# Three of seven gate/up tile pairs as seven products of halves (256 of 448 channels), with the roundings moved behind PSUM copies and the inverse transform split around the down projection

## The chip, the cores and the metric

The kernel runs on one core of a Trainium2 chip. The metric is the device time in microseconds. The kernel before was run three times: 1939.03, 1943.02 and 1942.74 us, median 1942.74 us. A further execution, taken with the hardware profiler, is the one whose trace is read here.

TensorE is called PE, VectorE DVE, ScalarE ACT, GpSimd POOL, and SP is the engine that issues the DMAs. "PEld" is PE's weight load.

## The reference

An input of 8192 rows by 448 channels goes through a spectral block and then a feed-forward block, each behind a modulated layer norm and with a gated residual:

```
h = _layernorm(x) * (1 + ca) + sa
x = x + ga * _A_ref(h, ...)                  # rfft2, two block-diagonal complex layers, softshrink, irfft2
h = _layernorm(x) * (1 + cb) + sb
x = x + gb * (gelu(h @ w_gate) * (h @ w_up)) @ w_down     # 448 -> 1792 -> 448
```

The case turns on the last line. It is done with float16 operands in two parts: a high part and the remainder, for weights and activations both, so one product takes three matmuls (high by high, high by low, low by high).

## The kernel before, in words

The first 380 us or so do the Fourier transform and the block-diagonal layers. What follows is one loop over `nch` = 32 chunks of 256 tokens (`for i in range(nch)`, L1275), each in 14 steps `k`.

**Gate and up.** A step is one 128-wide block of the hidden features. Steps 2t and 2t+1 (`q` = 0 and 1) make tile pair t, with t from 0 to 6; here it is called pair t. A step runs 20 matmuls of 256 columns (L1087): gate and up, each with ten weight blocks. The 448 channels lie in four weight blocks, the last of 64 rows. The products of those 64 rows with the low weights are taken together for two neighbouring pairs, eight matmuls of half height, at the end of the second step of the first of the two (`first_pair`, L1099).

**PSUM banks.** A first pair has two banks with the tag "pa", a second pair two with the tag "pb" (L1100 to L1103); each tag has two buffers, so the same two banks serve every second pair. The first write to the new "pa" banks is at the beginning of a first pair's steps, the first write to the new "pb" banks is among the eight half-height matmuls just named. Because a chunk has seven pairs, an odd chunk begins with a second pair and ends with one (pair 6 uses "pb"), and an even chunk ends with a first pair (pair 6 uses "pa").

**After a step.** `gate_up_out` (L1120) takes the gelu of the gate half on ACT (L1123, into one of two `gel` buffers) and multiplies by the up half on DVE (L1128); both read the PSUM bank, and the bank can be written again after the multiplication. For a second pair this follows each step, for a first pair both follow its second step. POOL then makes four sums of 128x128 (L1134 to L1137). `quantize` rounds the seven blocks to float16 on ACT (L1145) and takes the remainder on DVE (L1146).

**Down.** After step 2 of a chunk, `down` (L1158) runs the projection of the chunk before it, in seven products of halves instead of eight (147 matmuls of 224 columns), with sums on ACT, DVE and POOL, and stores the chunk.

**Preparation of chunk i+2.** The `hooks` table (L1201) spreads it over the steps of chunk i: the last inverse transform (L987 to L989, operands split into two parts by ACT and POOL, L105 and L107), the residual (L998 and L999), the row statistics (L1007), a reciprocal square root in 14 tiny DVE instructions (L116 to L125), the norm (L1036 and L1037), and the float16 packing (L1042, L1049 to L1051). Sixteen DMA transposes (L1057) follow a chunk later.

Each engine works through its instructions in the order in which the program wrote them, so an instruction that waits holds up what stands behind it on its engine.

Of the kernel before, what the change touches and what calls it, by code (L numbers as in the profile page):

```python
# [37 lines left out]
NTT = len(PKO)  # L38
LAM = 0.01
# [6 lines left out]
def spectral_geglu(ctx, tc, x, w1, b1, w2, b2, wg, wu, wd, cvec, wmod, cf1, cs2, cmi, cgm, out):  # L46
# [272 lines left out]
    with ExitStack() as bctx:  # L319
# [359 lines left out]
        def row_scales():  # L679
# [8 lines left out]
            pow2(sk, bnd)  # L688
# [50 lines left out]
        def scales1():  # L739
# [20 lines left out]
            pow2(sw, mxa)  # L760
# [122 lines left out]
        def load_g(i):  # L883
            g = ep.tile([128, CB, 128], F32, tag="g", name="g")
            dma(g, cgm[:, i * CB : (i + 1) * CB, :])
            xx = ep.tile([128, CB, D], F32, tag="xx", name="xx")
            dma(xx, xv[:, i * CB : (i + 1) * CB, :])
            nxt.setdefault(i, {}).update({"g": g, "xx": xx})
# [22 lines left out]

        def split_g(i):
            gh = ep.tile([128, CB, 128], F32R, tag="gh", name="gh")
            gl = ep.tile([128, CB, 128], F32R, tag="gl", name="gl")
            split(gh, gl, nxt[i]["g"], el=G)
            nxt[i]["g"] = gh, gl
# [32 lines left out]
    with ExitStack() as cctx:  # L949
# [7 lines left out]

        def load_d8(t):
            load_d(t, *(cp2.tile([128, n, HC], F32, tag=f"dr{n}", name="dr", bufs=2) for n in (3, 4)))
# [8 lines left out]
        def split_v(i, cs=slice(0, D)):  # L968
            n = nxt[i]
            if "vh" not in n:  # L970
                n["vh"] = cp.tile([128, CB, D], F32R, tag="vh", name="vh")
                n["vl"] = cp.tile([128, CB, D], F32R, tag="vl", name="vl")
            for b in each(i):
                split(n["vh"][:, b, cs], n["vl"][:, b, cs], n["v"][:, b, cs], el=G)

        def inverse(i, cs=slice(0, D), tag="pc"):
            nxt[i]["ps"] = []
            for b in range(CB):
                ps = bank(tag, "pi2")[:, cs]
                if i < 3:  # L980

                    T.matmul(ps, nxt[i]["g"][:, b], nxt[i]["v"][:, b, cs], start=True, stop=True)
                    nxt[i]["ps"].append(ps)
                    continue
                vh, vl = nxt[i]["vh"], nxt[i]["vl"]
                gh, gl = nxt[i]["g"]
                T.matmul(ps, gh[:, b], vh[:, b, cs], start=True, stop=False)  # L987
                T.matmul(ps, gl[:, b], vh[:, b, cs], start=False, stop=False)  # L988
                T.matmul(ps, gh[:, b], vl[:, b, cs], start=False, stop=True)  # L989
                nxt[i]["ps"].append(ps)  # L990

        def residual(i, cs=slice(0, D)):
# [383 lines left out]
```

## Time and profile before

| | before |
|---|---|
| median of three runs | 1942.74 us |
| the profiled execution | 1942.27 us |
| its span in the trace | 1940.5 us |
| mean granted PE clock | 0.995 |
| PE busy | 1901.1 us (98%) |
| DVE busy | 1108.7 us (57%) |
| ACT busy | 790.1 us (41%) |
| POOL busy | 1157.7 us (60%) |

The busy time is a mean over the whole program; the loop over chunks, from about 400 us on, is the part that the change touches. A timeline row gives the start, the time to the end of the last of the merged instructions, the engine, the line, and how many were merged; in brackets stands the idle time before, and what ended it. A group row gives the number of instructions, their busy time together, and the mean duration of one. Durations of one engine overlap by a little, so what an instruction costs in a dense row is the distance to the next start.

### The profile page before, as it was taken

The page shows a single profiled execution, that of the slowest core. Times are in us where ns is not written, and L with a number is a line of the kernel's source. Part 1 is how long each engine was busy: PE and PEld are TensorE (multiplying, and loading weights), DVE is VectorE, ACT ScalarE, POOL GpSimd, SP SyncE. Part 2 cuts the span into 40 slices and gives each one's busy share as a digit, 9 for nine tenths or more (in the row PEclk, how much of TensorE's full clock was granted, in tenths as well). Part 3 has the DMA queues.
Part 4 walks back from the last instruction along what each step waited for, and adds up shares of the span by engine and source line. Part 5 has one row for each costly group of instructions (what it writes and reads, how often), then busy time and mean ns, then how long its engine had stood idle before and what let it go on. Part 6 is the DMA issues. An engine that isn't in the chain of part 4 may idle for free.

```text
span 1940.5 us, 43566 instructions
## 1 busy us (share of the span) xinstructions
PE 1901.1 (98%) x17636; PEld 1694.6 (87%) x17636; DVE 1108.7 (57%) x2352; ACT 790.1 (41%) x1342; POOL 1157.7 (60%) x1466
## 2 busy tenths in 40 slices
PE   7899999899999999999999999999999999999998
PEld 3599999778888888888888888888888888888897
DVE  8677788786555555555555555555555555555533
ACT  5587888553333333333333333333333333333322
POOL 3157655256666666666666666666666666666644
PEclk9899999999999999999999999999999999999999
DMA  9999777541111111111111111111111111111000
GB/s 351 313 286 261 194 195 196 166 125 48 44 44 44 43 43 43 43 43 44 43 44 43 43 44 43 44 44 42 45 43 44 44 43 44 43 44 44 21 16 20
DMA packets 167330, 163.35 MB, mean 84 GB/s; under 512 B 87252, under 2 KB 145496, under 8 KB 167128
## 3 DMA queue, kind: packets, MB, share of 16 engines
q1 hardware_dynamic: 167128, 160.57, 28.3%
q8 instruction: 138, 2.26, 0.5%
q14 instruction: 64, 0.52, 0.1%
HBM read 97.44 MB, written 47.25 MB: 75 GB/s over the span
## 4 chain that ended last, share of the span: by engine, by line
PE 86%; DVE 4%; ACT 3%; issue 3%; DMA 2%; POOL 1%; SPq 1%; ACTq 0%; POOLq 0%; DVEq 0%
PE pgu L1087 53%; PE pdn L1155 8%; PE pdn L1153 8%; PE pdn L1154 8%; PE ps L202 2%; DVE y L463 2%; PE pi L989 1%; PE pi L988 1%; PE pi L987 1%; POOL yl L107 1%; DVE st L163 1%; ACT th L105 0%; DMA raw<-in_B_w_gate 0%; POOL tl L107 0%; ACT zh L376 0%
## 5 line engine op out<-in xcount | busy, mean ns | idle before, releaser
L1087 PE MATMUL pgu<-nt,wh 128*128 128x256 f16 x6272 | 834.2, 273 | 0.1
L1087 PEld LDWEIGHTS <-wh 128*128 128x128 f16 x6272 | 602.7, 98 | 98.5 <-issue 31.0
L1123 ACT ACTIVATE gel<-pgu,dg 128x256 f32<-128x256 f32 x448 | 200.3, 473 | 793.2 <-PE pgu L1087 756.1
L1087 PE MATMUL pgu<-nt,wl 128*128 128x256 f16 (+1 forms) x3584 | 501.3, 272 | 0.6 <-DVE x L1128 0.6
L1155 PE MATMUL pdn<-wd,ac 128*128 128x224 f16 x1568 | 406.1, 259 | 0.2 <-DVE ac L1146 0.2
L1153 PE MATMUL pdn<-wd,ac 128*128 128x224 f16 x1568 | 406.1, 259 | 0.0
L1154 PE MATMUL pdn<-wd,ac 128*128 128x224 f16 x1568 | 406.1, 259 | 0.0
L1134 POOL TENSOR_TENSOR x<-x 128x128 f32<-128x128 f32 x223 | 239.9, 1076 | 264.0 <-DVE x L1128 230.5
L1146 DVE SCALAR_TENSOR_TENSOR ac<-x,sa_act,ac 128x896 f16<-128x896 f32 (+1 forms) x225 | 308.2, 1370 | 81.9 <-ACT ac L1145 81.9
L1087 PEld LDWEIGHTS <-wl 128*128 128x128 f16 (+1 forms) x3584 | 297.8, 97 | 57.6 <-issue 24.4
L1128 DVE TENSOR_TENSOR x<-pgu,gel 128x256 f32<-128x256 f32 x448 | 179.6, 418 | 278.7 <-ACT gel L1123 278.0
L1145 ACT ACTIVATE ac<-x,sa_act 128x896 f16<-128x896 f32 (+1 forms) x225 | 232.9, 1035 | 46.5 <-POOL x L1137 44.5
L1190 POOL TENSOR_TENSOR o<-u,p 128x224 f32<-128x224 f32 x32 | 21.0, 657 | 291.6 <-DVE u L1189 291.6
L1135 POOL TENSOR_TENSOR x<-x 128x128 f32<-128x128 f32 x223 | 158.1, 709 | 17.5
L1155 PEld LDWEIGHTS <-ac 128*128 128x128 f16 x1568 | 153.4, 98 | 0.5 <-DVE ac L1146 0.5
L1154 PEld LDWEIGHTS <-ac 128*128 128x128 f16 x1568 | 153.4, 98 | 0.4
L1153 PEld LDWEIGHTS <-ac 128*128 128x128 f16 x1568 | 153.4, 98 | 0.4
L107 POOL TENSOR_TENSOR yl<-y,yh 128x448 fp32r<-128x448 f32 x63 | 78.9, 1252 | 75.6 <-ACT yh L105 63.0
L463 DVE SCALAR_TENSOR_TENSOR y<-pm,t 64x224 f32<-64x224 f32 x256 | 99.5, 389 | 41.3 <-ACT t L455 37.4
L1136 POOL TENSOR_TENSOR x<-x 128x128 f32<-128x128 f32 x223 | 113.0, 507 | 0.0
L1137 POOL TENSOR_TENSOR x<-x 128x128 f32<-128x128 f32 x223 | 109.2, 490 | 0.0
L107 POOL TENSOR_TENSOR tl<-tr,th 128x896 f16<-128x896 f32 x30 | 57.3, 1909 | 69.5 <-DMA tr<-td 38.2
(281 smaller groups left out, 2728.4 us busy)
## 6 DMA issues: line engine op xcount, KB each, us to landing
tr<-td SPq DMA_DIRECT2D x64, 224.0 KB, 4.3
vd<-us SPq DMA_DIRECT2D x64, 224.0 KB, 3.3
xx<-in_A_x SPq DMA_DIRECT2D x32, 448.0 KB, 3.3
v<-vd SPq DMA_DIRECT2D x63, 224.0 KB, 2.7
out<-x SPq DMA_DIRECT2D x31, 448.0 KB, 2.6
xt<-in_A_x SPq DMA_DIRECT2D x15, 896.0 KB, 14.8
td<-xt SPq DMA_DIRECT2D x48, 224.0 KB, 4.3
nt<-pk SPq DMA_TRANSPOSE x480, 2.3
```

What stands on the lines that cost most here:

```text
L107: (el or V).tensor_tensor(lo, src, h, ALU.subtract)
L463: V.scalar_tensor_tensor(y[ri * 64 : ri * 64 + 64, gi], pv[si, ri], LAM, tv[si, ri], op0=ALU.add, op1=ALU.min)
L1087: T.matmul(pgu[i, t, q][:, pr * H : (pr + 1) * H], w[rows, tw, f0 : f0 + 128], nts[i][rows, tn, :], start=start, stop=stop, skip_group_che ...
L1123: S.activation(gl, ps[:, :H], AF.Gelu_apprx_tanh, scale=dg)
L1128: V.tensor_tensor(dst, ps[:, H : 2 * H].rearrange("p (b c) -> p b c", b=2), gl.rearrange("p (b c) -> p b c", b=2), ALU.mult)
L1134: e.tensor_tensor(s1, a21, a22, ALU.add)
L1135: e.tensor_tensor(s2, s1, a11, ALU.subtract)
L1145: S.activation(ac[:, 0, k], x[:, k], AF.Copy, scale=sc)
L1146: V.scalar_tensor_tensor(ac[:, 1, k], x[:, k], sc, ac[:, 0, k], op0=ALU.mult, op1=ALU.subtract)
L1153: T.matmul(ps, ac[:, 0, ka], wds[t][:, 0, kb], start=t == 0, stop=False)
L1154: T.matmul(ps, ac[:, 0, ka], wds[t][:, 1, kb], start=False, stop=False)
L1155: T.matmul(ps, ac[:, 1, ka], wds[t][:, 0, kb], start=False, stop=t == NP - 1)
```

## The change

For pairs 2, 4 and 6, from chunks 3, 4 and 5 on (`SP`), the part of gate and up over the first two weight blocks (256 channels) is written as a 2x2 block product, two halves of the channels by two halves of the features and of the tokens, and taken in seven products instead of eight. Each product is 128x128x128 for gate and for up, so its matmuls have 128 columns. The other two weight blocks stay as they were (`rest`, with 256 columns). The core of it:

```diff
+        def gate_up_s1(i, t, first_pair):
+            pv = bank("pc", "px").rearrange("p (x r c) -> p x r c", x=2, r=2)
+            x, u = pv[:, 0], sums["u"]
+            sp_product(i, t, x, 0, 0, start=True)
+            sp_product(i, t, pv[:, 1], 3, 3)
+            S.copy(u[:, :, 0], x)
+            rest(i, t, 0, 0, first_pair, 2)
+            sp_product(i, t, x, 4, 6)
+            S.copy(u[:, :, 1], x)
+            rest(i, t, 0, 1, first_pair, 2)
+            o = outs(i, t, 0)
+            sp_product(i, t, o[:, :, 0], 1, 1, stop=not first_pair)
+            sp_product(i, t, x, 5, 4, stop=True)
+            S.copy(u[:, :, 2], x)
+            sp_product(i, t, o[:, :, 1], 2, 5, stop=not first_pair)
+        def gate_up_s2(i, t, first_pair):
+            for pr in range(2):
+                rest(i, t, 1, pr, first_pair, 2)
+            sp_product(i, t, outs(i, t, 1)[:, :, 0], 6, 2, stop=not first_pair)
...
             if not first_pair:
+                gate_up_sums(i, t, q)
                 gate_up_out(i, t, q)
...
+        def gate_up_sums(i, t, q):
+            if seven(i, t):
+                u, o = sums["u"], outs(i, t, q)
+                if q == 0:
+                    V.tensor_tensor(o, o, u[:, :, 0::2], ALU.add)
+                    y = sums["px"][:, 1].unsqueeze(2).broadcast_to([128, 2, 2, 128])
+                    V.tensor_tensor(u[:, :, 1:3], y, u[:, :, 1:3], ALU.add)
+                else:
+                    V.tensor_tensor(o, o, u[:, :, 1:3], ALU.add)
...
-                if k % 2 == 1 and i + k > 1 and (i, k) != (nch - 1, NFT - 1):
-                    quantize(*((i, k // 2 - 1) if k > 1 else (i - 1, NP - 1)))
+                for p in [p for p in unrounded if 2 * p + 3 + (p >= 2 * NP) == i * NFT + k]:
+                    quantize(*divmod(p, NP))
...
         hooks = {
-            0: [(1, transposes_dma)],
-            3: [(2, split_g), (2, split_v)],
-            6: [(2, inverse)],
-            7: [(2, residual)],
-            8: [(2, stats2)],
-            9: [(2, rsqrt_part, 5)],
+            0: [(1, transposes_dma, range(4))],
+            3: [(1, s_transposes), (2, inverse1, 0), (2, split_v, 1)],
+            4: [(2, residual, slice(0, D), [0])],
+            5: [(2, stats2, slice(0, D), [0])],
+            6: [(2, inverse1, 1)],
+            7: [(2, residual, slice(0, D), [1])],
+            9: [(2, stats2, slice(0, D), [1]), (2, rsqrt_part, 5)],
             10: [(2, rsqrt_part, 9)],
             11: [(2, norm2, 0)],
             12: [(2, norm2, 1)],
-            13: [(2, pack_hi), (2, pack_lo)],
+            13: [(2, pack_hi), (2, pack_lo), (2, s_sums)],
         }
```

One product (`sp_product`) is six matmuls of 128 columns: gate and up, three each. A pair has 42 of them, 36 in its first step (with `px`, a bank of tag "pc", for the partial sums that more than one output needs) and six in its second. ACT copies the running partial sum out of `px` three times (`u`), and PE adds to `px` after the first and after the second copy. DVE adds the copies to the output banks, two instructions of 128x512 after the first step and one after the second; for a first pair all three follow the second step.

Further: POOL makes four sums and one remainder for the activations of the seven products, and ACT one copy (`s_sums`, `s_pack`); eight more DMA transposes per chunk carry them (`s_transposes`). `quantize` comes one step later, at even steps instead of odd ones. The inverse transform of a chunk is taken one half of the chunk at a time (`inverse1`), the first after step 3, the second after step 6; the splitting of its operands begins inside `down`. The norm writes into the tile that held the transform's input, so the loads for chunk i+2 move from the steps 0 and 1 to step 2, and the load of `x` behind `down`. The weights' sums are made once per pair, in chunks 2 to 4. Two scale factors become smaller by four, with no change in work.

The first place is DVE, from the multiplication after step 11 of an odd chunk to the multiplication after step 13. `pgu` is an output bank, `x` with a number a pair's tile (25719 and 28330 are pair 5, 25756 and 28393 pair 6), `ac` the float16 result, `dr` the copies `u`. Before:

```order
L1128 TENSOR_TENSOR x_25719<-pgu,gel 128x256
L1146 SCALAR_TENSOR_TENSOR ac<-x_25611,sa_act,ac 128x896
L1036 SCALAR_TENSOR_TENSOR n_25731<-x_25584,cmv,cb_r 128x448
L1037 SCALAR_TENSOR_TENSOR n_25731<-n_25731,rcy,sb_r 128x448
L1128 TENSOR_TENSOR x_25756<-pgu,gel 128x2x128
L1036 SCALAR_TENSOR_TENSOR n_25731<-x_25584,cmv,cb_r 128x448
L1037 SCALAR_TENSOR_TENSOR n_25731<-n_25731,rcy,sb_r 128x448
L1128 TENSOR_TENSOR x_25756<-pgu,gel 128x256
```

And the same stretch after the change:

```order
L1271 TENSOR_TENSOR x_28330<-pgu,gel 128x256
L1039 SCALAR_TENSOR_TENSOR v<-x_28075,cmv,cb_r 128x448
L1040 SCALAR_TENSOR_TENSOR v<-v,rcy,sb_r 128x448
L1257 TENSOR_TENSOR pgu<-pgu,dr 128x512
L1259 TENSOR_TENSOR dr<-px,dr 128x2x256
L1271 TENSOR_TENSOR x_28393<-pgu,gel 128x2x128
L1289 SCALAR_TENSOR_TENSOR ac<-x_28228,sa_act,ac 128x896
L1039 SCALAR_TENSOR_TENSOR v<-x_28075,cmv,cb_r 128x448
L1040 SCALAR_TENSOR_TENSOR v<-v,rcy,sb_r 128x448
L1261 TENSOR_TENSOR pgu<-pgu,dr 128x512
L1271 TENSOR_TENSOR x_28393<-pgu,gel 128x256
```

Three additions of 128x512 have come between (L1257, L1259, L1261), and the remainder for pair 4 (`x_25611`, `x_28228`) has moved from behind pair 5's multiplication to behind pair 6's first one.

The second place is ACT in the same odd chunk, from the gelu of pair 5 to the packing after step 13. Before:

```order
L1123 ACTIVATE gel<-pgu,dg 128x256 x2
L1145 ACTIVATE ac<-x_25611,sa_act 128x896
L1123 ACTIVATE gel<-pgu,dg 128x256 x2
L1145 ACTIVATE ac<-x_25719,sa_act 128x896
L1042 CAST pk<-n_25731 128x2x448
```

After:

```order
L1266 ACTIVATE gel<-pgu,dg 128x256 x2
L1210 COPY dr<-px 128x2x128
L1213 COPY dr<-px 128x2x128
L1218 COPY dr<-px 128x2x128
L1266 ACTIVATE gel<-pgu,dg 128x256
L1288 ACTIVATE ac<-x_28228,sa_act 128x896
L1266 ACTIVATE gel<-pgu,dg 128x256
L1045 CAST pk<-v 128x2x448
```

The three copies out of `px` stand behind both gelus of pair 5 and ahead of the gelu and the rounding that follow.

More of the change, by code (lines that the diff above doesn't have):

```diff
@@ L995, in residual @@
             x1 = x1t[i][:, :, cs]
-            for b in range(CB):
+            for b in bs:
                 e = V if i < 3 else G
@@ L1241, in spectral_geglu @@
         }
+        for i in (1, 2):
+            x1t[i] = x1_tile(i)
+        nxt[0]["n"] = x1t[2]
         inverse(0, halves[0], "pa")
@@ L1274, in spectral_geglu @@
         V.tensor_scalar(gb_r, gb_r, ds_d, None, op0=ALU.mult)
+        unrounded = range(nch * NP - 2)
         for i in range(nch):
```

204 lines of the change are left out of this document (158 added, 46 removed).

## The prediction

> **What bounds the kernel now.** I read the stages first, then PE's timeline, then what PE waits for. In the loop over chunks the columns after the window's length are the busy time of PE, PEld, DVE, ACT and POOL:
>
> ```profile
> 1000.00:1200.00 200.00, 200.00 (x1913) 178.64 (x1911) 107.28 (x220) 64.88 (x108) 129.50 (x167) 1.00 0.16 44
> ```
>
> PE has no gap at all there, at full granted clock (1.00), while DVE and ACT are busy for 54% and 32%. So time is won by fewer PE columns, and lost as soon as any engine makes PE wait. The end of an odd chunk on PE:
>
> ```profile
> 1050.22 0.94 PE L1087 MATMUL pgu<-nt,wh 128*128 128x256 f16 x7
> ...
> 1054.60 0.93 PE L1087 MATMUL pgu<-nt,wh 128*128 128x256 f16 x7
> ...
> 1058.64 1.03 PE L1087 MATMUL pgu<-nt,wl 128*128 128x256 f16 x11
> 1059.61 0.94 PE L1087 MATMUL pgu<-nt,wh 128*128 128x256 f16 x7
> ```
>
> Step 12 begins at 1050.22, the next (even) chunk two steps later at 1054.60: a step is 2.19 us for 20 matmuls, 0.109 us each. The row at 1058.64 holds three whole matmuls (to 1058.97) and the eight half-height ones, 0.08 us each. From the third of them, at 1059.13, PE writes the "pb" banks that pair 6 used. DVE at the same time:
>
> ```profile
> 1047.15 0.63 DVE L1007 BATCH_NORM_STATS2 cst<-x 128x6 f32<-128x448 f32 x1 [0.47 <-POOL x L999]
> 1047.70 0.30 DVE L1010 BATCH_NORM_AGGREGATE cmv<-cst 128x2 f32<-128x6 f32 x2
> 1047.91 0.39 DVE L1128 TENSOR_TENSOR x<-pgu,gel 128x256 f32<-128x256 f32 x1
> 1048.22 1.14 DVE L1146 SCALAR_TENSOR_TENSOR ac<-x,sa_act,ac 128x896 f16<-128x896 f32 x1
> 1049.28 0.42 DVE L116 TENSOR_SCALAR rcve<-cmv 128x2 f32<-128x2 f32 x1
> ...
> 1052.35 0.75 DVE L1128 TENSOR_TENSOR x<-pgu,gel 128x256 f32<-128x256 f32 x2
> 1053.01 1.14 DVE L1146 SCALAR_TENSOR_TENSOR ac<-x,sa_act,ac 128x896 f16<-128x896 f32 x1
> 1054.07 0.88 DVE L1036 SCALAR_TENSOR_TENSOR n<-x,cmv,cb_r 128x448 f32<-128x448 f32 x1
> 1054.98 0.76 DVE L1037 SCALAR_TENSOR_TENSOR n<-n,rcy,sb_r 128x448 f32<-128x448 f32 x1
> 1055.67 0.41 DVE L1128 TENSOR_TENSOR x<-pgu,gel 128x256 f32<-128x256 f32 x1
> ...
> 1057.59 0.42 DVE L1128 TENSOR_TENSOR x<-pgu,gel 128x256 f32<-128x256 f32 x1
> ```
>
> The mean of 54% hides this: from 1047.15 on DVE never stops, and pair 6's last multiplication ends at 1058.01, only 1.1 us ahead of PE's write at 1059.13. An even chunk has its pair 6 in "pa", written next at the beginning of step 2 (first row DVE, second PE):
>
> ```profile
> 1105.09 0.74 DVE L1128 TENSOR_TENSOR x<-pgu,gel 128x256 f32<-128x256 f32 x2
> ```
> ```profile
> 1107.60 0.93 PE L1087 MATMUL pgu<-nt,wh 128*128 128x256 f16 x7
> ```
>
> Its multiplications end at 1105.83: 1.8 us to spare. That PE does wait for this multiplication when it is late, the list of PE's waits shows once:
>
> ```profile
> PE pgu L1087 <- DVE x L1128: 0.6, 1, 0.6
> ```
>
> **What the change saves.** Per changed pair 24 matmuls of 256 columns go and 42 of 128 columns come. Such matmuls with a weight load each exist already, in the Fourier stage (24 of them, first and last shown) and in the first transposes, with full 128x128 weights:
>
> ```profile
> 250.84 0.22 PE L368 MATMUL ps<-s,th 128*112 128x128 f16 x1
> ...
> 252.13 0.22 PE L370 MATMUL ps<-s,tl 128*112 128x128 f16 x1
> ```
> ```profile
> 383.59 0.61 PE L1069 MATMUL ptr<-ident,pk 128*128 128x128 f16 x8
> ```
>
> 1.29 us over 23 intervals is 0.056 us each; the eight transposes give (0.61 - 0.22)/7 = 0.056 too. So a pair costs 42 x 0.056 = 2.36 us in place of 24 x 0.109 = 2.62, a saving of 0.26 us. Pairs 2, 4 and 6 are changed from chunks 3, 4 and 5 on: 29 + 28 + 27 = 84 pairs, **-21.8 us**. A changed pair's first step is then 36 x 0.056 + 8 x 0.109 = 2.89 us, its second 6 x 0.056 + 8 x 0.109 = 1.21.
>
> The Trainium skill, "TensorE: Matmul & The Clock Gate", section "Back-to-back issue gap", speaks against this: in a stream of weight loads and matmuls it gives about 81 ns for N=128, and 56 ns only for an isolated gap. By it a pair would take 42 x 0.081 = 3.40 us, a loss of 0.79 us, an estimate of +66 us for 84 pairs; the rows above, which are such streams, measure 56 ns, and the sum goes by them.
>
> **What the sums on DVE cost.** No 128x512 addition is in the trace. The nearest rows are group rows (count, total, mean ns):
>
> ```profile
> L1128 DVE TENSOR_TENSOR x<-pgu,gel 128x256 f32<-128x256 f32 x289 | 115.6, 417 | 174.0 <-ACT gel L1123 173.5
> L1036 DVE SCALAR_TENSOR_TENSOR n<-x,cmv,cb_r 128x448 f32<-128x448 f32 x42 | 37.5, 894 | 0.0
> L998 DVE TENSOR_TENSOR x<-pi,ga_r 128x448 f32<-128x448 f32 x42 | 24.1, 615 | 0.0
> ```
>
> Two-operand work on PSUM goes from 417 ns at 256 elements to 615 at 448, so 512 gives 0.68 us, with 0.60 to the next start (rows end 0.08 later than the next begins). Bounds: 0.615, the shorter row as it is, and 894 x 512/448 = 1.02, the dearest form of that length. I take 0.68, the same operation on the same operands.
>
> A changed bank also needs its steps in turn: sum, gelu, multiplication; while DVE's multiplication waits for the gelu, all that stands behind it on DVE waits too, the statistics of chunk i+2 first. One gelu, one rounding and what follows on DVE:
>
> ```profile
> 1034.78 0.47 ACT L1123 ACTIVATE gel<-pgu,dg 128x256 f32<-128x256 f32 x1 [1.31 <-PE pgu L1087]
> 1035.16 1.03 ACT L1145 ACTIVATE ac<-x,sa_act 128x896 f16<-128x896 f32 x1
> ```
> ```profile
> 1035.29 0.42 DVE L1128 TENSOR_TENSOR x<-pgu,gel 128x256 f32<-128x256 f32 x1 [1.36 <-ACT gel L1123]
> 1036.22 1.76 DVE L1146 SCALAR_TENSOR_TENSOR ac<-x,sa_act,ac 128x896 f16<-128x896 f32 x1 [0.51 <-ACT ac L1145]
> ```
>
> From the gelu's start it is 0.51 us to the multiplication, 1.44 to the remainder. With 0.05 us to hand over, the multiplication starts 0.68 + 0.05 + 0.51 = 1.24 us after its sum began, the remainder 2.17.
>
> Odd chunk, time from DVE's first sum of pair 4 (0.20 us after PE ended step 8): sums, multiplication at 1.24, remainder (pair 2) at 2.17, to 3.23; second sum, multiplication at 4.46, to 4.79; statistics of one half 0.67, the 14 instructions of the root 3.07 (1049.28 to 1052.35), remainder 1.06 (1048.22 to 1049.28), two multiplications 0.66: 10.25; norm 1.60 (1054.07 to 1055.67): 11.85; pair 6: sums, multiplication, remainder at 14.02, to 15.08; norm: 16.68; last sum, multiplication at 17.91, done at 18.4. PE, from the same zero: -0.20, step 9 1.21, step 10 2.19, step 11 2.82, steps 12 and 13 4.10, the next two steps 4.38, three half-height matmuls 0.24, and ACT's copies (below) 0.1: it wants the bank at 14.9. **It waits 3.5 us**, each in the 13 odd chunks 5 to 29 (chunk 31 prepares nothing and nothing follows).
>
> Even chunk, from the end of step 9: three sums 1.80, second multiplication at 2.43, to 2.76; statistics 0.67, root 3.07, remainder 1.06, two multiplications 0.66: 8.22; norm, remainder, norm: 12.48; three sums: 14.28; the multiplication ends at 14.7. PE wants that bank at -0.20 + 4.38 + 2.89 + 1.84 (step 13 with the half-height ones) + 4.38 = 13.3. **It waits 1.4 us** in the 12 even chunks 6 to 28. Together 13 x 3.5 + 12 x 1.4 = **+62.3 us**.
>
> **ACT's copies.** Behind a waiting matmul stands all of PE. PE adds to `px` again after 12 x 0.056 + 4 x 0.109 = 1.11 us. Ahead of the copy stand the gelus of the step before, and at step 4 also two copies for the inverse:
>
> ```profile
> 1050.21 0.84 ACT L1123 ACTIVATE gel<-pgu,dg 128x256 f32<-128x256 f32 x2 [3.39 <-PE pgu L1087]
> ```
> ```profile
> L105 ACT CAST vh<-v 128x896 fp32r<-128x896 f32 x20 | 18.8, 941 | 0.0
> L105 ACT CAST gh<-g 128x256 fp32r<-128x256 f32 x20 | 7.9, 397 | 0.0
> L1176 ACT COPY p<-pdn 128x224 f32<-128x224 f32 x21 | 7.3, 346 | 76.9 <-PE pdn L1155 76.9
> ```
>
> Two gelus leave ACT free after some 0.75 us; the copy, 346 ns at 224 and so about 0.37 at 256, is through at 1.15 with the hand-over: a wait of 0.04. At step 4 the halves of the casts (0.29 and 0.56 us by the slope of the two rows, less overlap) put it at 1.30: 0.19. The second copy has 0.33 + 0.44 + 0.33 us and needs less. 29 x 0.19 plus the rest is **+7 us**; from 0, if ACT runs ahead, to 17, if each copy is 0.1 us later.
>
> **The moves.** DMA transposes, loads, POOL's extra sums and the remainder of the weights lie beside PE: POOL is busy 65% in the first row and PE meets its results only in the two halves of the inverse, as before. `quantize` for pair 6 now ends just about when `down` wants it, 36 matmuls in. I put **+3 us** for these, from 0 to 8. The weights' sums come once, in chunks 2 to 4, inside that.
>
> Sum, against the profiled execution's 1942.3 (0.5 us under the median): 1942.3 - 21.8 + 62.3 + 7 + 3 = **1993 us**. With the cheap bound for a sum the two waits are 3.2 and 1.0 us and the total without ACT's 1975; with the dear one 4.9 and 3.4 us, and with 17 and 8 us it is 2050.
>
> **The rivals.** *DVE is in time.* Then only the columns and ACT's copies count: 1942.3 - 21.8 + 7 = 1928 us, faster. For it: DVE is half idle on average. Against it: in the rows from 1047.70 to 1057.59 it has no idle time at all, and the change puts six additions more between steps 8 and 13. It decides at 3.5 us less on DVE between steps 8 and 13, or if PE's write needs less than the multiplication of the old bank.
>
> *DVE is late by half.* If a sum takes 0.3 us less than I think, the odd chunk's wait is 3.5 - 4 x 0.3 = 2.3 us and the even one's gone (six sums): 1942.3 - 21.8 + 30 + 7 = 1957 us.
>
> *Weight loads set the pace of short matmuls.* A load lasts 98 ns in the profile's groups:
>
> ```profile
> L1087 PEld LDWEIGHTS <-wh 128*128 128x128 f16 x6272 | 602.7, 98 | 98.5 <-issue 31.0
> ```
>
> If they did not overlap, a pair would take 42 x 0.098 = 4.1 us, 1.5 more than before: +126 us, less some DVE lateness, about 2095. The transposes at 0.056 us, with weights of that size, are against it. The page of the Trainium skill named above gives the same cause in its section "Back-to-back issue gap": the spacing is set by the load and the matmul together.
>
> **How the numbers follow.** Late DVE as worked out 0.68, in time 0.17, late by half 0.11, weight loads 0.04. The forecast is 1993 us, its own range 1975 to 2050. Down to 1950 and up to 2050 the range takes in the first and the third case and leaves out about 2 in 10. No change within 0.2% (4 us, about what a measurement of this kernel can tell) lies only between the second and third case: 0.03, taken from the third. Faster 0.17, slower 0.80.
>
> **What would show it.** In the changed profile: matmuls of 128 columns 0.056 us apart; PE waiting for DVE at the half-height matmuls after step 1 of even chunks, some 3.5 us, and at the beginning of step 2 of odd chunks, some 1.4; DVE without a gap from step 9 to the next chunk's step 1; short waits of `px` for ACT, longest at step 4. A PE without waits on DVE, or sums well below 0.6 us, would make the prediction wrong.

## The result and the profile after

| | before | after |
|---|---|---|
| median | 1941.81 us (4 runs) | 2061.70 us (4 runs, 2059.77 to 2064.80) |
| the profiled execution, its span | 1942.27, 1940.5 us | 2064.80, 2063.0 us |
| mean granted PE clock | 0.995 | 0.983 |

The changed kernel is slower: the ratio is 1.062, with an interval of 1.0602 to 1.0640. That is 120 us more, where 51 were forecast, and outside the range. The direction and the main wait were foreseen, the size was not.

First the same stretch of the loop as before. The columns after the length are the busy time of PE, PEld, DVE, ACT and POOL, and behind them the granted clock. The second row is 3 us right after one of the waits shown below:

```profile
1000.00:1200.00 200.00, 186.78 (x1965) 166.53 (x1963) 109.92 (x215) 73.84 (x145) 127.29 (x184) 0.99 0.18 48
1112.60:1115.60 3.00, 3.00 (x16) 2.07 (x15) 1.82 (x3) 0.74 (x3) 3.00 (x5) 0.50 0.15 33
```

PE now stands still for 13 of 200 us, and in the second row it runs at half clock. What it waits for (total, times, longest, in us):

```profile
PE pgu L1112 <- DVE x L1271: 67.1, 33, 3.0
PE pdn L1296 <- ACT p L1319: 13.8, 15, 1.2
...
PE pdn L1298 <- DVE ac L1289: 6.7, 7, 1.7
...
PE px L1191 <- ACT dr L1210: 4.2, 9, 0.7
...
PE pi L991 <- DVE x L1002: 3.2, 5, 1.4
```

The first row is the wait that the prediction worked out, at the two output banks. Its two places on PE: the half-height matmuls after step 1 of an even chunk (twice, 104 us apart), and the beginning of step 2 of an odd one (1059.12). The last row but one is seven matmuls in 1.50 us, 0.214 us each in place of 0.109:

```profile
1007.51 0.48 PE L1112 MATMUL pgu<-nt,wl 64*128 64x256 f16 x5 [2.78 <-DVE x L1271]
...
1059.12 0.92 PE L1112 MATMUL pgu<-nt,wh 128*128 128x256 f16 x7 [1.75 <-DVE x L1271]
...
1111.36 0.48 PE L1112 MATMUL pgu<-nt,wl 64*128 64x256 f16 x5 [2.78 <-DVE x L1271]
...
1113.39 1.70 PE L1112 MATMUL pgu<-nt,wh 128*128 128x256 f16 x7
1114.89 0.84 PE L1112 MATMUL pgu<-nt,wl 128*128 128x256 f16 x3
```

DVE in the odd chunk ahead of the wait at 1007.51, from the first sum of pair 4 to pair 6's last multiplication:

```profile
989.65 0.70 DVE L1257 TENSOR_TENSOR pgu<-pgu,dr 128x512 f32<-128x512 f32 x1 [0.71 <-ACT dr L1218]
990.38 0.69 DVE L1259 TENSOR_TENSOR dr<-px,dr 128x512 f32<-128x512 f32 x1
...
1001.20 0.69 DVE L1257 TENSOR_TENSOR pgu<-pgu,dr 128x512 f32<-128x512 f32 x1
...
1005.74 0.69 DVE L1261 TENSOR_TENSOR pgu<-pgu,dr 128x512 f32<-128x512 f32 x1
1007.03 0.42 DVE L1271 TENSOR_TENSOR x<-pgu,gel 128x256 f32<-128x256 f32 x1 [0.60 <-ACT gel L1266]
```

A sum lasts 0.69 to 0.70 us (0.68 was taken), and the chain from 989.65 to 1007.45 is 17.8 us (18.4 was worked out). The 128-column matmuls of pair 2, twelve in a row, and PE's first short wait behind them:

```profile
1027.15 0.28 PE L1191 MATMUL px<-nt,wh 128*128 128x128 f16 x2
...
1027.78 0.22 PE L1191 MATMUL px<-nt,wl 128*128 128x128 f16 x1
1027.83 0.49 PE L1112 MATMUL pgu<-nt,wh 128*128 128x256 f16 x3
1028.16 0.27 PE L1112 MATMUL pgu<-nt,wl 128*128 128x256 f16 x1
1028.45 0.50 PE L1191 MATMUL px<-nt,dr 128*128 128x128 f16 x6
```

The twelfth starts 0.63 us after the first: 0.057 us each (over all 3192 such distances at full clock the mean is 55.9 ns). The product into `px` at 1028.45 starts 0.29 us after the matmul ahead of it, where 0.11 is usual: 0.18 us lost, though the list of waits names few of these. Last, POOL and then ACT at the beginning of `down` in an odd chunk:

```profile
1059.84 0.46 POOL L1277 TENSOR_TENSOR x<-x 128x128 f32<-128x128 f32 x1 [3.73 <-DVE x L1271]
```
```profile
1067.75 0.62 ACT L1069 CAST pks<-v 128x512 f16<-128x512 f32 x1 [5.01 <-POOL v L1064]
1068.27 0.34 ACT L1319 COPY p<-pdn 128x224 f32<-128x224 f32 x1
```

POOL, idle for 3.73 us, gets pair 6 only when DVE has multiplied it, and then makes that pair's sums, the packing and the sums of halves. The copy of down's first product stands behind the rounding of the halves' sums, and that waits 5 us for POOL: this is the second row of the list of waits.

**Where the 120 us are.** In the loop alone, from its first matmul of gate and up to PE's last matmul, the profiled executions take 1549.5 and 1674.2 us: 124.7 more. I compared the distances between the starts of neighbouring matmuls in both traces, took what exceeds the usual 0.108 us wherever a distance is over 0.15, and counted matmuls at half clock apart:

| | forecast | measured |
|---|---|---|
| 84 pairs with fewer columns (worked out, at 0.056 and 0.109 us a matmul) | -21.8 | -21.8 |
| among gate and up: PE waits for the banks | +62.3 | +66.0 |
| PE ahead of the third product into `px` | +7 | +20.0 |
| other distances around `px` | - | +4.9 |
| the inverse in two halves | in +3 | +9.0 |
| down waits for ACT's first copy | in +3 | +17.0 |
| down waits for DVE's remainder | in +3 | +7.5 |
| the first transposes wait less | - | -2.5 |
| half clock: 12 stretches, 51.2 us in the loop (before: one of 3.4) | - | +21.3 |
| sum | +51 | +121.4 |

3 us stay unassigned.

### The profile page after: what moved, and what is told of

Same layout as the page of the kernel before. It is cut to its first block, busy times and chain, and to the rows that moved or that the text cites. A ratio compares the mean times of both kernels' runs of the same rounds, so it can differ in the third digit from the quotient of the medians.

```text
span 2063.0 us, 47911 instructions
## 1 busy us (share of the span) xinstructions
PE 1931.4 (94%) x19148; PEld 1706.8 (83%) x19148; DVE 1233.8 (60%) x2616; ACT 898.1 (44%) x1693; POOL 1202.1 (58%) x1693
## 4 chain that ended last, share of the span: by engine, by line
PE 37%; DVE 23%; POOL 14%; ACT 8%; issue 7%; DMA 7%; SPq 4%; POOLq 0%; ACTq 0%; DVEq 0%
PE pgu L1112 12%; PE pdn L1296 5%; PE pdn L1298 5%; PE pdn L1297 4%; DVE ac L1289 4%; ACT gel L1266 3%; PE px L1191 3%; DVE x L1271 2%; DVE pgu L1261 2%; SPq L1082 2%; DVE pgu L1257 2%; ACT ac L1288 2%; DMA out<-x 2%; POOL x L1311 2%; POOL o L1310 2%
## 5 line engine op out<-in xcount | busy, mean ns | idle before, releaser
L1112 PE MATMUL pgu<-nt,wh 128*128 128x256 f16 x4928 | 694.9, 277 | 27.7 <-DVE x L1271 27.5
L1112 PEld LDWEIGHTS <-wh 128*128 128x128 f16 x4928 | 467.6, 99 | 105.2 <-issue 53.6
L1112 PE MATMUL pgu<-nt,wl 128*128 128x256 f16 (+1 forms) x2912 | 446.3, 276 | 39.9 <-DVE x L1271 39.6
L1296 PE MATMUL pdn<-wd,ac 128*128 128x224 f16 x1568 | 407.4, 260 | 14.1 <-ACT p L1319 13.8
L1289 DVE SCALAR_TENSOR_TENSOR ac<-x,sa_act,ac 128x896 f16<-128x896 f32 (+1 forms) x225 | 274.2, 1219 | 144.1 <-ACT ac L1288 87.2
L1277 POOL TENSOR_TENSOR x<-x 128x128 f32<-128x128 f32 x223 | 121.0, 543 | 373.7 <-DVE x L1271 369.2
L1112 PEld LDWEIGHTS <-wl 128*128 128x128 f16 (+1 forms) x2912 | 235.4, 98 | 95.3 <-issue 63.0
L1288 ACT ACTIVATE ac<-x,sa_act 128x896 f16<-128x896 f32 (+1 forms) x225 | 232.6, 1034 | 14.7 <-POOL x L1280 13.8
L1279 POOL TENSOR_TENSOR x<-x 128x128 f32<-128x128 f32 x223 | 142.1, 637 | 0.0
L1278 POOL TENSOR_TENSOR x<-x 128x128 f32<-128x128 f32 x223 | 116.4, 522 | 17.5
L1280 POOL TENSOR_TENSOR x<-x 128x128 f32<-128x128 f32 x223 | 124.0, 556 | 0.0
L1191 PEld LDWEIGHTS <-wh 128*128 128x128 f16 x1344 | 109.3, 98 | 16.3 <-issue 11.9
```

Source lines behind the costliest of these rows:

```text
L1112: T.matmul(pgu[i, t, q][:, pr * H : (pr + 1) * H], w[rows, tw, f0 : f0 + 128], nts[i][rows, tn, :], start=start, stop=stop, skip_group_che ...
L1191: T.matmul(o[:, pr], weight(pr, l), act(la), start=start and pr == 0 and n == 0, stop=stop and n == 2, skip_group_check=True,)
L1277: e.tensor_tensor(s1, a21, a22, ALU.add)
L1279: e.tensor_tensor(s3, a11, a21, ALU.subtract)
L1280: e.tensor_tensor(s4, a12, s2, ALU.subtract)
L1288: S.activation(ac[:, 0, k], x[:, k], AF.Copy, scale=sc)
```

## The experiments

Each ratio is to the kernel before, run beside it on the same chip. "Half clock" is the number of stretches at half the granted clock inside the loop and their length together, from the record of the clock in the trace.

| run | median us | ratio, 95% interval | half clock |
|---|---|---|---|
| no_sums | 1946.26 | 1.0033 (1.0021 to 1.0044) | 2, 6.8 us |
| moves_only | 1947.24 | 1.0034 (1.0021 to 1.0047) | 2, 6.8 |
| pair2_only | 1950.38 | 1.0049 (1.0033 to 1.0066) | 2, 6.8 |
| pack_after_p1 | 2316.28 | 1.1932 (1.1914 to 1.1949) | 37, 283.3 |
| wait_dose | 1953.93 | 1.0075 (1.0060 to 1.0090) | 1, 3.4 |
| copy_first | 2095.34 | 1.0810 (1.0792 to 1.0828) | 5, 17.1 |
| block_after_p1 | 2055.71 | 1.0600 (1.0584 to 1.0616) | 9, 34.1 |
| root_on_pool | 2090.31 | 1.0782 (1.0759 to 1.0804) | 25, 92.2 |
| root_short | 2018.02 | 1.0396 (1.0376 to 1.0416) | 1, 6.8 |
| pairs_24 | 1991.16 | 1.0262 (1.0245 to 1.0279) | 3, 10.2 |
| pair6_only | 1989.11 | 1.0252 (1.0234 to 1.0270) | 2, 6.8 |
| wait_dose2 | 1976.17 | 1.0185 (1.0170 to 1.0200) | 4, 17.1 |
| even_gaps | 2063.54 | 1.0633 (1.0614 to 1.0651) | 14, 64.9 |
| pair2_even | 1947.01 | 1.0036 (1.0023 to 1.0048) | 2, 6.8 |
| pairs_23_even | 2060.50 | 1.0629 (1.0614 to 1.0645) | 10, 44.4 |
| rounding_odd | 2143.81 | 1.1053 (1.1011 to 1.1095) | 16, 61.4 |

### Which part costs it: no_sums, moves_only, pair2_only

```diff
 def gate_up_sums(i, t, q):          # no_sums
-            if seven(i, t):
+            if False:
```

> This kernel leaves out the three additions of partial sums on DVE in each changed pair, so that its outputs lack those sums; matmuls, ACT's copies and all moves stay. Theory (most of the loss is DVE's lateness at the two output banks, some 67 us of PE's waits, and the half-speed clock that follows the longer of them, some 20 us; the rest is ACT's copies, the rounding of the halves' sums ahead of down's first copy, and the first chunks): PE's waits for DVE at the half-height matmuls after step 1 and at the start of step 2 are gone, the mean clock is back at 0.995, and the time is 1942 - 22 (columns) + 16 (first copies) + 15 (down's first copy and the first chunks), about 1950 us, 1940 to 1970. Rival, the moves cost most of it: bank waits go but 1990 to 2010 us stay. Rival, the short matmuls themselves cost it: over 2000 us, with no waits to see.

```diff
-SP = {2: 3, 4: 4, 6: 5}
+SP = {}                             # moves_only
```

> No pair takes seven products (all columns as before), but everything that was moved for them stays: the rounding two steps later, the inverse in halves, the sums of halves of the normed rows, their rounding and transposes, the later loads; the weights' sums are gone. Theory: the moves cost little by themselves, 1942 + 3 to 10 us, about 1948 us, and down's first copy is in time because DVE and so POOL are not late. Rival, the moves make the loss: 1980 us or more.

```diff
-SP = {2: 3, 4: 4, 6: 5}
+SP = {2: 3}                         # pair2_only
```

> Only pair 2 takes seven products (29 pairs in place of 84), in the middle of the chunk. Theory: DVE still has idle time after pair 2 and is through with its three sums before the crowded end of the chunk, so that no bank wait appears; 1942 - 7.5 (columns) + 6 (first copies) + 6 (moves), about 1946 us. Rival, DVE's backlog is carried to the chunk's end wherever it arises: three sums of 0.6 us, 1.8 us more at the odd chunk's bank, which has 1.1 us to spare: 15 x 0.7 us and the copies, 1960 us or more.

All three came where the theory had them, pair 2 alone 4 us above its figure: 1946, 1947 and 1950 us. PE's waits without the sums:

```profile
PE pgu L1112 <- DVE x L1271: 6.3, 6, 2.6
...
PE pdn L1298 <- DVE ac L1289: 4.8, 4, 1.7
...
PE pdn L1296 <- ACT p L1319: 0.7, 3, 0.2
```

The bank waits go from 67.1 to 6.3 us, and with them go down's wait for ACT's first copy (13.8 to 0.7) and the half clock, though nothing was done about either. So 115 of the 120 us hang on 252 additions, and the moves by themselves cost 7 us. These 7 us fall in the loop's first three chunks: counted from the first matmul of gate and up, moves_only is 7.4 us behind the kernel before at the 800th, 518 us into the program, and 7.0 at the 9850th, near its end. In the steady loop the moves cost nothing. Without the sums the columns' 22 us are still not won: `px` takes as much.

### What is late behind DVE: pack_after_p1, block_after_p1

```diff
-                    s_pack(i + 1)                       # at step 2, ahead of down
-                    if i + 2 < nch:
-                        load_v(i + 2)
-                        load_g(i + 2)
                     transposes_dma(i + 1, range(4, NTT))
...
             S.copy(p4, product(i, bank("pd", "pdn"), 2, 5))
+            s_pack(i + 2); load_v(i + 3); load_g(i + 3)      # conditions left out
```

> The changed kernel, but the rounding of the sums of halves (and the loads behind it) is issued behind down's copies of its first and third product and not ahead of them. Theory: PE's wait for ACT's copy of down's first product (13.8 us in 15 waits, and some of the clock behind it) goes and nothing takes its place: 2045 us, 2038 to 2052. Rival, that wait only passes the time that DVE's lateness sets: it comes back at the next bank and the time stays at 2060.

Neither: 2316 us. The edit had also put the loads behind eight more transposes on SP, and the chunk's operands came late, at the inverse:

```profile
PE pi L991 <- ACT vh L107: 205.1, 28, 9.1
```

SP's queue says why (first pair of rows this run, second pair the changed kernel): the loads of `v` now stand behind sixteen transposes in place of eight, which take 20.75 us in place of 10.84. The rounding that was moved is not what they wait for: it ran from 1103.26, and its remainder on POOL to 1105.12.

```profile
1094.44 20.75 SPq L1082 DMA_TRANSPOSE nt<-pk  x16
1115.30 1.03 SPq L900 DMA_DIRECT2D v<-vd  x2
```
```profile
1060.16 10.84 SPq L1082 DMA_TRANSPOSE nt<-pk  x8
1071.11 1.03 SPq L900 DMA_DIRECT2D v<-vd  x2
```

The second try kept the order of loads and transposes and moved the whole block behind the first copy (conditions left out):

```diff
             S.copy(p1, product(i, b1, 0, 0, [NP - 1]))
+            s_pack(i + 2); load_v(i + 3); load_g(i + 3)
+            transposes_dma(i + 2, range(4, NTT))
```

> The changed kernel; the rounding of the sums of halves, with the loads and transposes behind it in their old order, is issued behind ACT's copy of down's first product instead of ahead of it (the run before this moved the loads behind the transposes as well, and that was what it measured). Theory: PE's waits for that copy go (13.8 us in 15 waits), the loads start under 1 us later, 2047 us. Rival, the inverse at step 3 has no time to spare for its loads: waits for the copies of v at the inverse take the place of it, 2060 us or more.

2055.7 us, between the two expectations and nearer the rival's. PE's waits:

```profile
PE pgu L1112 <- DVE x L1271: 72.3, 41, 3.1
...
PE pi L991 <- DVE x L1002: 5.7, 7, 1.2
```

The wait for the copy is gone (13.8 us to none), but the bank waits rise by 5.2 and the inverse's by 2.5: PE comes earlier to a bank that is no earlier. Of the 13.8 us only 6 were left by the medians, 4 by the ratios, whose intervals overlap.

### Price of a PE wait: wait_dose, wait_dose2

Here the kernel before is run with DVE held up by repeated instructions. wait_dose2 repeats pair 4's rounding, wait_dose pair 5's:

```diff
-                V.scalar_tensor_tensor(ac[:, 1, k], ...)
+                for _ in range(1 + ((i - 5) // 2 % 7 if i % 2 and i > 4 and t == 4 and i < nch - 1 else 0)):
+                    V.scalar_tensor_tensor(ac[:, 1, k], ...)
```

> The kernel before, all columns and moves as they were; only DVE's rounding of pair 5 is repeated (same result) 0 to 6 times more in the odd chunks 5 to 29, in turn (chunk 5: 0, 7: 1, ... 17: 6, 19: 0, ...). So PE is made to wait for DVE at the half-height matmuls, by 1.06 us a repeat less the 1.1 us to spare: 0, 0, 1.0, 2.1, 3.1, 4.2 and 5.3 us, 26 us in all over the 13 chunks. Theory (a wait of about 3 us or more costs again as much as half of a 3.4 us stretch at half clock, a shorter one only itself): half-clock stretches in the chunks with 4, 5 and 6 repeats alone, 5 of them at 1.7 us, together 1940 + 26 + 9 = 1975 us. Rival, the clock stretches of the changed kernel come from its short matmuls and not from the waits: no half-clock stretch here, 1966 us.

The repeats stood behind pair 6's multiplications and not ahead of them, so the banks were in time and down waited for DVE's remainder (12.4 us in 12 waits). It tells the price all the same: 14.5 us more for 12.4 us of waits and one stretch at half clock (1.7). That stretch follows the longest wait, 3.00 us; the next longest is 2.0 us and has none behind it:

```profile
1262.47 0.37 PE L1156 MATMUL pdn<-wd,ac 128*128 128x224 f16 x1 [3.00 <-DVE ac L1147]
1262.63 0.39 PE L1154 MATMUL pdn<-wd,ac 128*128 128x224 f16 x1
1262.82 0.39 PE L1155 MATMUL pdn<-wd,ac 128*128 128x224 f16 x1
```

> The kernel before with DVE's rounding of pair 4, not of pair 5, repeated 0 to 6 times more in the odd chunks 5 to 29 (the repeats of pair 5 fell behind pair 6's multiplications on DVE and held up only down). Here they stand ahead of them: waits of 0, 0, 1.0, 2.1, 3.1, 4.2 and 5.3 us at the half-height matmuls. Theory (a PE wait of about 3 us or more brings a stretch of 3.4 us or more at half clock, a shorter one none; no short matmuls are here): stretches in the chunks with 4, 5 and 6 repeats, five in all; 1940 + 26 + 5 x 1.7 = 1975 us. Rival, the stretches need the short matmuls: none here, 1966 us.

1976.17 us against 1975 expected. The chunks with three repeats (first two rows) and with four, and the granted clock behind the one with five:

```profile
962.34 0.27 PE L1087 MATMUL pgu<-nt,wl 64*128 64x256 f16 x1 [0.49 <-DVE x L1128]
963.98 0.48 PE L1087 MATMUL pgu<-nt,wl 64*128 64x256 f16 x5 [1.38 <-DVE x L1128]
...
1062.13 0.27 PE L1087 MATMUL pgu<-nt,wl 64*128 64x256 f16 x1 [1.55 <-DVE x L1128]
1063.78 0.48 PE L1087 MATMUL pgu<-nt,wl 64*128 64x256 f16 x5 [1.38 <-DVE x L1128]
```
```profile
1167.00:1170.40 3.40, 3.40 (x18) 2.42 (x17) 1.40 (x4) 1.82 (x4) 3.32 (x7) 0.50 0.09 19
```

No short matmul is in this kernel, so the half clock comes from the waits. Four repeats brought a stretch in one chunk of two, five in both, six a double one; three, none.

### Dose and place: root_short, root_on_pool, pairs_24, pair6_only

```diff
-        for it in range(3):
+        for it in range(1 if tag == "rc" else 3):      # root_short
```

> The changed kernel without the second and third Newton iteration of the root in the chunks of the loop, so that its rows are normed with a coarse root: six small instructions fewer on DVE, 0.2 us each, 1.2 us per chunk, nothing else. Theory (DVE's work after step 8 passes straight on to PE, and the half-clock stretches hang on waits of about 3 us): the odd chunks' wait falls from 3.0 to 1.8 us, the even ones' from 1.9 to 0.7, 25 x 1.2 = 30 us, down's first copy comes earlier by the same (up to 14 us), and the half-clock stretches go (54.8 us of them, up to 24 us of time): 2061 - 30 - 5 to 14 - 15 to 24 = 1993 to 2011, about 2000 us; more is won than DVE is spared (36 us in 30 chunks). Rival, the stretches belong to the short matmuls: 2025 us.

2018 us: 44 us less for some 36 us of DVE's time (six instructions of 0.2 us in each chunk). The bank waits fell by 32 us and the half clock behind them went, as the theory said; PE waits for down's first copy as long as before, and for the inverse longer, which is why it is 2018 and not 2000:

```profile
PE pgu L1112 <- DVE x L1271: 34.8, 29, 2.1
PE pdn L1296 <- ACT p L1319: 13.9, 15, 1.2
...
PE pi L991 <- DVE x L1002: 8.0, 11, 1.3
```

That the wait for the copy stays has a reason that the traces show. PE's step 2 of an odd chunk and POOL's sums are released by the multiplications of the same pair 6. Wherever PE has waited at that bank at all, down goes on behind its first copy 9.55 to 9.57 us after step 2 began: after 1.9 us of waiting in the changed kernel, 0.9 here, 0.2 to 1.1 with pair 6 alone (below). POOL's and ACT's way from the multiplication to the copy is then 1.3 us longer than PE's, however late DVE is (0.7 in one chunk of each of these runs).

```diff
+            if tag == "rc":                              # root_on_pool
+                steps += [lambda: G.tensor_tensor(t, y, y, ALU.mult),
+                          lambda: G.tensor_tensor(t, t, ve, ALU.mult),
+                          lambda: (G.tensor_scalar(t, t, 1.5, None, op0=ALU.add), G.tensor_tensor(y, t, y, ALU.mult))]
+                continue
```

> The changed kernel; the three Newton iterations of the root, nine of its fourteen small instructions on DVE, run on POOL (twelve there). DVE's chain from pair 4 to the bank gets 9 x 0.22 = 2.0 us shorter in each chunk. Theory: the odd chunks' wait falls from 3.0 to 1.0 us and the even ones' from 1.9 to nothing, 13 x 2.0 + 12 x 1.9 = 49 us, the half-clock stretches behind the 3 us waits go too, some 20 us, and down's first copy is in time: 1980 us, 1970 to 1995. Rival, POOL is late instead (it sums what the roundings need) and DVE's norm waits for POOL: 2045 to 2070 us.

The rival, and worse: 2090 us, bank waits 93.6 us. DVE's norm now waits for POOL in the middle of the crowd, and what stands behind it waits too:

```profile
1063.67 0.67 DVE L1046 SCALAR_TENSOR_TENSOR v<-x,cmv,cb_r 128x448 f32<-128x448 f32 x1
1066.68 0.86 DVE L1047 SCALAR_TENSOR_TENSOR v<-v,rcy,sb_r 128x448 f32<-128x448 f32 x1 [2.34 <-POOL rcy L128]
```

Work taken off a late engine is not time taken off it, if it must wait for the result.

```diff
-SP = {2: 3, 4: 4, 6: 5}
+SP = {2: 3, 4: 4}                   # pairs_24; pair6_only: {6: 3}
```

> Pairs 2 and 4 take seven products, pair 6 does not (57 pairs). Theory (the loss comes from the sums that stand after step 8, and a wait is only what exceeds the time to spare, 1.1 us in odd and 1.8 us in even chunks): pair 4's sums and the steps between them put some 2.4 us more on DVE, PE itself comes 0.3 us earlier: 1.3 to 1.6 us of wait in 14 odd chunks, nothing to 0.6 in the even ones, no half-clock stretch: 1950 (pair 2 alone) + 13 x 1.5 + 5 = 1970 us, 1955 to 1985. Rival, each pair costs alike (119 us by three, 40 each): 2020 us.

> Pair 6 alone takes seven products, from chunk 3 on (29 pairs). Theory: its three sums stand right before the two banks' last multiplications; 1.8 to 2.4 us more on DVE against 1.1 and 1.8 us to spare: 0.7 to 1.3 us of wait in odd chunks, 0 to 0.6 in even ones, no half-clock stretch: 1947 (moves) - 7.5 + 10 (first copies) + 15 x 1.0 + 14 x 0.3 = 1968 us, 1955 to 1980; with the run of pairs 2 and 4 and that of pair 2 alone less than the 114 us by which all three differ from the moves, since a wait is what exceeds the time to spare. Rival, each pair costs alike: 1985 us.

1991 and 1989 us, both some 20 us above the theory and outside its ranges; pair 6's time lies nearer to the rival's. The costs over moves_only are 44 and 42 us, with pair 2 alone at 3; by place it is pairs 4 and 6 that cost, not each alike, and 44 and 42 are together less than the 114 of all three, as the theory had it. But the theory looked for the lateness at the banks, and there is little there. With pairs 2 and 4 it comes out at the inverse, whose bank DVE's residual of the other half has not yet read:

```profile
PE pi L991 <- DVE x L1002: 14.5, 12, 2.6
...
PE pdn L1296 <- ACT p L1319: 8.0, 15, 0.6
PE pgu L1112 <- DVE x L1271: 7.0, 9, 2.6
```

With pair 6 alone it comes out at down's first copy, at full size since PE has waited a little at the bank, and nearly as much as at the banks:

```profile
PE pgu L1112 <- DVE x L1271: 15.7, 25, 2.6
PE pdn L1296 <- ACT p L1319: 14.5, 14, 1.2
```

### ACT's copies and roundings: copy_first, even_gaps, rounding_odd, and pairs that are in time

```diff
             sp_product(i, t, x, 0, 0, start=True)      # copy_first
+            S.copy(u[:, :, 0], x)
             sp_product(i, t, pv[:, 1], 3, 3)
-            S.copy(u[:, :, 0], x)
```

> The changed kernel; only ACT's first copy out of px is issued ahead of the second product into the other half of the same bank, not behind it, so that it is released six short matmuls (0.34 us) earlier. Theory: PE's short waits at the third product, about 0.2 us in 84 pairs, go for the most part: 10 to 16 us less, 2048 us. Rival, those waits lie beside DVE's lateness: what PE gains ahead of the late bank it waits longer there, and the time stays within 5 us of 2061.

Neither: 2095 us. The second product goes to the other half of the same bank, and the program makes it wait for ACT's read of the first half, at all 84 pairs:

```profile
PE px L1191 <- ACT dr L1209: 65.2, 84, 1.5
```

So PE stands still for 0.78 us a copy with nothing between (65.2 by 84), and by the distance between the starts loses 0.94; in the changed kernel the matmuls between hide all but 0.24 of that. (The Trainium skill, "PSUM — Partial Sum Buffer", section "PSUM bank collisions raise a hardware error", says that an engine's read and TensorE's write in one bank and the same partitions must be kept apart, whichever columns they touch; that agrees with the order enforced here, and no run here tries the two at once.)

```diff
             rest(i, t, 0, 0, first_pair, 2)            # even_gaps; the line o = outs(i, t, 0) moves up too
+            rest(i, t, 0, 1, first_pair, 2)
             sp_product(i, t, x, 4, 6)
             S.copy(u[:, :, 1], x)
-            rest(i, t, 0, 1, first_pair, 2)
             sp_product(i, t, o[:, :, 0], 1, 1, stop=not first_pair)
+            sp_product(i, t, o[:, :, 1], 2, 5, stop=not first_pair)
             sp_product(i, t, x, 5, 4, stop=True)
             S.copy(u[:, :, 2], x)
-            sp_product(i, t, o[:, :, 1], 2, 5, stop=not first_pair)
```

> The changed kernel; in a changed pair's first step PE's work is put in another order, so that at least 0.67 us of other matmuls stand between each copy's release and the next product into px (both rests ahead of the third product, both products into the output bank ahead of the last); the same matmuls. Theory (ACT's first copy is a term of its own, some 0.2 us in each of 84 pairs, 16 us): those waits go; since PE then reaches the late banks earlier, about half is given back: 2053 us, 2045 to 2062, with the waits for the bank up. Rival, the copies cost nothing of their own: 2061 us and the same gaps.

The gaps ahead of `px` went (2.2 us of 20.0 are left), and the time stayed: 2063.5 us. All was given back, at the banks, 75.9 us in place of 67.1, with 13.7 us more at half clock, and at the inverse, 5.3 in place of 3.2:

```profile
PE pgu L1112 <- DVE x L1271: 75.9, 48, 3.1
```

> Pair 2 alone in seven products, with the order of PE's work as in the run above. Theory: against pair 2 alone in the old order (1950) the first copy's wait of 0.2 us in 29 pairs goes and DVE is in time: 1944 us, so 7.5 us of columns less half a us of start. Rival, nothing of the saving arrives: 1950.

With that order and pair 2 alone 1947.0 us: 3 us under the old order (the intervals overlap), and no better than the moves without any seven products. Expected was 1944.

> Pairs 2 and 3 in seven products (29 + 28), in that order of PE's work. Theory (what ruins the saving is only that the sums stand late in the chunk): the sums of pair 3 in steps 6 and 7 are done before the crowded end, 1947 (moves) - 57 x 0.26 = 1932 us, 1930 to 1942, at or below the kernel before. Rival, DVE's backlog of pair 3 is carried on to the inverse's bank and to down's first copy, as with pairs 2 and 4: 1955 to 1990 us.

The rival, 2060 us, and above its range, but not where it looked. Both waits are pair 3's. Its first copy out of `px` stands on ACT behind the gelus of pair 2, which wait for DVE's sums of pair 2; and its first product waits for DVE's residual, in 13 of the 28 chunks, since `px` and the inverse share their banks.

```profile
PE px L1191 <- ACT dr L1210: 47.4, 28, 2.9
PE px L1191 <- DVE x L1002: 33.2, 13, 3.3
```

```diff
-                for p in [p for p in unrounded if 2 * p + 3 + (p >= 2 * NP) == i * NFT + k]:
+                for p in [p for p in unrounded if 2 * p + 3 == i * NFT + k]:      # rounding_odd
```

> The changed kernel with the roundings back at the odd steps, as before the change. Theory: each pair's rounding (1.04 us on ACT) then stands ahead of the first copy of the step behind it, so PE waits some 0.8 us more at most changed pairs, 50 to 65 us; this gives DVE time, and the waits at the banks and their half-clock stretches shrink by 40 to 70 us: 2040 to 2080, about 2062 us, with the waits at px above 50 us in place of 4. Rival, the roundings' place matters for DVE alone: the remainder of pair 2 is out of the crowd, 25 us less and no more at px, 2035 us.

2144 us, above the range of the theory, with its mechanism: PE waits at `px` and no longer at the banks.

```profile
PE px L1191 <- ACT dr L1210: 130.8, 83, 3.6
...
PE pgu L1112 <- DVE x L1271: 11.3, 16, 2.6
```

So the roundings' place behind the copies is worth some 82 us to this change. None of the sixteen beats the kernel before.

## Why the prediction was wrong

**Right.** What a short matmul costs, 0.056 us (the weight loads set no pace, and that rival falls); what a sum costs, so that "late by half" falls too; DVE's chain of 17.8 us; the two places of the bank waits. Their total came out by luck in part: 2.78 and 1.75 us in the rows above, 3.5 and 1.4 forecast, so one was too long and the other too short; 66 us in all, 4 of them from the moves, against 62.3. The rival "DVE is in time" falls by the list of waits. The moves by themselves: 3 us with a bound of 8 were put, 7 us measured.

**Wrong, the step that failed:** the +3 us for the moves, with the reason that they "lie beside PE" and that PE meets POOL's results "only in the two halves of the inverse, as before". It measured 31 us (9.0 + 17.0 + 7.5 - 2.5). Of the 71 us by which the measured sum exceeds the forecast, 28 are this term, 21 the clock, 18 ACT's copies, and under 4 the banks. The prediction let DVE's lateness reach PE at two banks alone and priced a microsecond of waiting at a microsecond. DVE's lateness had more exits. DVE multiplies pair 6 late, so POOL sums late, so ACT rounds late, and down's first copy stands behind that on ACT: 17 us. The inverse waits for DVE's residual: 4 of its 9 us, since 5 are there in moves_only as well. These lay beside PE, as the sentence has it, while DVE was in time, and ceased to when it was not: down's wait and the half clock vanish with the sums. The prediction counted ACT's rounding and POOL as hidden without naming what would be late once DVE was.

A part of the failed step has nothing to do with the sums: down's third matmuls wait for the remainder, 6.7 us in the list, 4.8 without the sums, 1.7 (once) with pair 2 alone and none in moves_only. It grows with the number of changed pairs; by the order of the program DVE's rounding of the weights' sums stands ahead of that remainder in chunks 3 to 5, where the longest of these waits lie. The prediction had it inside its +3.

**Missing: the clock.** A wait of near 3 us is followed by a stretch at half clock, 21 us in all. wait_dose2 shows that it needs no short matmuls, only waits; root_short shows that sparing DVE some 36 us wins 44.

**Too small: ACT's copies,** +7 for 20. The forecast had 0.19 us at step 4 and 0.04 at the other pairs; the 84 pairs lose 0.24 us on average, and 0.19 without the sums (15.8 us counted in the same way). The forecast started the copy when ACT is free of the gelus, 0.75 us after the step began. In no_sums every one of the 84 copies starts 0.256 us after the start of the twelfth short matmul, to which the trace gives 0.219 us, whenever ACT was free. With eleven distances of 0.056 us ahead of it, 0.37 for the copy and 0.05 to PE that makes 1.295 us, where PE comes at 1.11: 0.19 us at every pair. As a term of its own this is of no weight, though: even_gaps took it away and won nothing while DVE was late. Terms that lie one behind the other on the way to the same late bank do not add up.

**Open:** why pairs_24 loses so much at the inverse was read from its waits and not tried by itself; nor did any run shorten the way from pair 6's multiplication over POOL and ACT to down's copy (block_after_p1 moved the copy ahead of it, and PE waited elsewhere).

## What to carry to other kernels

When an edit makes an engine late, follow everything that stands behind it, over two further engines and to each place where the matmul engine meets their results; removing one of the waits then mostly makes the next one longer. A kernel at 98% of PE with DVE half idle can still lose 6% to 0.7 us additions, if they fall where DVE has 1 us to spare. Take away the suspected work first (here the additions, one line): it gave 115 of 120 us in one run, while four repairs of single waits gave 6 us at best or made it worse.

## What the runs showed of the clock

Unexpected: the granted clock goes by fixed windows. In each of the 17 traces taken after the prediction every half-clock stretch starts on one grid of 3.413 us and lasts a multiple of it (the last one ends with the trace). To count idle time I let a matmul last as long as the usual distance to the next of its kind. Of the windows in the loop in which PE ran at full clock and stood still for at least a quarter, all 134 with PE idle for 64% or more (2.2 us) were followed by a window at half clock, none of the 543 below 57% (1.9 us), and 13 of the 50 between. (With the matmuls' ends as the profile models them the shares are lower, and the two kinds mix between 47 and 59%.) Two equal waits of 2.78 us fit this: the one that ends at 1111.36 leaves PE idle for 75% of one window and is followed by half clock; the one that ends at 1007.51 is split into 60% of one window and 33% of the next, and is not. A half-clock window costs up to half of itself, 1.7 us.

The Trainium skill, "TensorE: Matmul & The Clock Gate", section "HAM oscillation — how this bites in real kernels", puts the limit at idle gaps of above some 3.4 us and the cost at half of the throttled time. The cost agrees; the limit does not, since a single wait of 3.00 us or even 2.78 brings it here, and the measurement decides.
